# A clustered attention and two gated MLPs on one core: the first head pair's preparation laid out anew

## The chip, the cores and the metric

The kernel runs on one core of a Trainium2 chip. Its engines have a queue each: TensorE (PE, with its weight loads listed apart as PEld), VectorE (DVE), ScalarE (ACT), GpSimd (POOL), and SyncE (SP), which issues the DMAs here. An engine takes its own instructions in the order in which they were written, and waits for another by semaphores. The metric is the device time of one execution in microseconds (us).

## What is computed

Attention among tokens of one cluster, for 2 batches, 8 heads, 768 tokens and 64 columns per head, and behind it two MLPs on the 1536 x 512 result.

```python
q_assign = argmax(einsum('bhsd,hcd->bhsc', q_n, c_n))      # 16 centroids per head, all normalised
k_assign = argmax(einsum('bhsd,hcd->bhsc', k_n, c_n))
mask = q_assign[:, :, :, None] == k_assign[:, :, None, :]
scores = where(mask, scale * q @ k.T, -1e9)
attn = softmax(scores)
x = (attn @ v) as 1536 x 512
x = (sigmoid(x @ w_gate) * (x @ w_val)) @ w_out            # d_ff 1536
out = relu(x @ w_in2) ** 2 @ w_out2                        # d_ff 2048
```

## The kernel before

All operands of the matmuls are split into a high and a low part of a shorter float type (fp32r), so that two or three matmuls together keep nearly the accuracy of fp32. The engines' orders are written out by hand: the order of the calls in the program is the order on each queue.

**Attention** goes over 8 head pairs (2 batches x 4), a pair being two heads whose 64 columns together fill the 128 partitions. A pair has 12 units, `n` = 0 to 95 over all pairs; a unit is 128 query rows of one head against all 768 keys. Unit `n` takes: `scores` (four matmuls, two for each of two passes `a`, into a PSUM buffer `s`, of which there are two), the row maximum on DVE (`TENSOR_REDUCE`, L935, called the reduce below), the exponential with its row sum on ACT (L956), a 1e-9 added to the sum on POOL (L970), its reciprocal on DVE (L874), the normalisation on POOL (L875). Three units later (`LAG`) its six 128x128 blocks are transposed on PE (L821), copied to fp32r by ACT (`pt_hi`, L823), and DVE takes the rest (`pt_lo`, L829). The matmuls with `v` follow.

**The mask** is part of the score matmuls: the second pass has 16 more rows for each head, which hold a one-hot code of the token's cluster for `k` and minus a large number for `q`. So each pair needs a **preparation** before its units (`prep`): q and k are loaded with tokens on partitions and transposed (`tk0`, `tk1`, `tq0`, `tq1`: k or q, first or second half of the tokens); ACT writes the high part and DVE the low one (L568, L569); the similarities to the centroids are made (`sims`, L618: eight matmuls with the centroids as weights, then a copy by ACT, L624) and transposed back (`back`, L635; the tile `tot` sums their high and low part, L645); the best cluster is chosen by five DVE operations over `tot` (L656 to L679, the last writes the one-hot tile `oh`); `oh` is transposed and written as mask rows. `stack` issues DMAs that put parts of a head on the partitions where the score matmuls want them. The centroids are normalised once, at the start, and lie in `cen`.

The preparation of pair 0 stands before the loop, with some steps of pair 1's between (`STEPS` and `SECOND_STEPS` say at which unit a step of the next pair stands). `keep_warm` puts transposes of the identity on PE, whose result nobody reads. Head 0's mask rows of pair 0 are written straight to their place from PSUM by ACT and DVE (`first_mask`, L712 and L715); head 1's go to the tile `row` and from there by DMA, and are needed from unit 6 on.

What a step leaves to ACT and DVE (its `post`) is emitted later, when `drain` is called.

**The MLPs** are matmuls of 512 columns, with weights that are loaded as 64-bit floats and decoded on DVE and ACT.

## Time and profile before

| | |
|---|---|
| time, three runs | 820.73, 821.72, 821.74 us (median 821.72) |
| the profiled execution's own time | 821.03 us |
| its span, first to last instruction | 819.2 us |
| busy in the span | PE 803.1 us (98%), PEld 689.8, DVE 625.9 (76%), ACT 442.1 (54%), POOL 214.2 (26%) |
| chain that ended last | PE 80%, DVE 12%, POOL 3%, ACT 2%, DMA 1% |

The span and the profiled execution's time are of the same execution; 1.8 us lie outside the span. The busy time is an average over the opening, the attention (to about 275 us) and the MLPs. The chain is found by going back from the last instruction, at each step to what released it; where it names an engine, work on this engine, and nothing else, was what the end waited for.

### The profile page before, as it was taken

To read this page: it belongs to the slowest core of one execution; us is meant where nothing else is said; L and a number is where in the kernel's file an instruction comes from. 1 tells how busy PE (TensorE), PEld (TensorE's weight loads), DVE (VectorE), ACT (ScalarE), POOL (GpSimd) and SP (SyncE) were. 2 spreads that over 40 slices of the span, in tenths; PEclk is the share of its full clock that TensorE was granted. 3 is DMA by queue.
4 is the path that set the end of the run, shared out by engine and by line. 5 is a ranking of instruction groups with operands and counts; after the bars stand their busy time and mean duration, and the time that the engine had idled before them with its cause. 6 is when DMAs were issued, how large, how long until landed. Compare 5 with 4: busy or idle time off the path is not lost.

```text
span 819.2 us, 11691 instructions
## 1 busy us (share of the span) xinstructions
PE 803.1 (98%) x4097; PEld 689.8 (84%) x4097; DVE 625.9 (76%) x1144; ACT 442.1 (54%) x889; POOL 214.2 (26%) x349
## 2 busy tenths in 40 slices
PE   7899999999999999999999999999999999999998
PEld 6789989999998788888888888888888888888886
DVE  5899999999898378657878767769784787788233
ACT  5888889888896223532332223336745733642530
POOL 4668989988884200000000000000000000000000
PEclk9999999999999999999999999999999999999999
DMA  8465455364321122122221212202222212221012
GB/s 190 108 144 144 102 136 121 92 143 96 78 77 44 52 71 95 51 71 68 94 77 52 78 52 78 78 0 89 66 78 77 78 52 77 78 78 52 0 52 102
DMA packets 63274, 67.01 MB, mean 82 GB/s; under 512 B 28624, under 2 KB 54224, under 8 KB 63216
## 3 DMA queue, kind: packets, MB, share of 16 engines
q1 hardware_dynamic: 63216, 66.27, 29.3%
q8 instruction: 32, 0.52, 0.3%
q14 instruction: 26, 0.21, 0.1%
HBM read 45.12 MB, written 3.15 MB: 59 GB/s over the span
## 4 chain that ended last, share of the span: by engine, by line
PE 80%; DVE 12%; POOL 3%; ACT 2%; issue 1%; DMA 1%; SPq 0%; POOLq 0%; ACTq 0%; DVEq 0%
PE bank_b L427 18%; PE bank_a L350 13%; PE bank_a L351 13%; PE bank_a L349 13%; PE bank_a L427 9%; DVE pt_lo L829 4%; PE t L821 4%; DVE nm L935 3%; PE s L803 3%; PE o L839 2%; PE o L840 2%; POOL p L875 1%; PE t L618 1%; PE t L563 1%; PE o L888 1%
## 5 line engine op out<-in xcount | busy, mean ns | idle before, releaser
L350 PE MATMUL bank_a<-x_lo,w 128*128 128x512 f32 x480 | 187.0, 389 | 0.9 <-POOL x_lo L870 0.9
L349 PE MATMUL bank_a<-x_hi,w 128*128 128x512 f32 x480 | 186.9, 389 | 0.0
L351 PE MATMUL bank_a<-x_hi,w 128*128 128x512 f32 x480 | 186.9, 389 | 0.0
L393 DVE TENSOR_TENSOR slo<-act,shi 128x512 fp32r<-128x512 f32 x84 | 57.9, 689 | 66.8 <-ACT shi L392 60.3
L350 PEld LDWEIGHTS bank_a<-x_lo,w 128*128 128x128 f32 x480 | 90.1, 188 | 19.7 <-POOL x_lo L870 1.2
L349 PEld LDWEIGHTS bank_a<-x_hi,w 128*128 128x128 f32 x480 | 90.1, 188 | 18.8 <-POOL x_hi L868 0.2
L351 PEld LDWEIGHTS bank_a<-x_hi,w 128*128 128x128 f32 x480 | 90.1, 188 | 18.8
L829 DVE TENSOR_TENSOR pt_lo<-t,pt_hi 128x384 fp32r<-128x384 f32 x192 | 96.7, 546 | 5.4 <-ACT pt_hi L823 5.4
L875 POOL TENSOR_SCALAR p<-p,nm,ones 128x768 f32<-128x768 f32 x96 | 94.8, 988 | 15.7 <-DVE nm L874 15.3
L956 ACT ACTIVATE p<-s,nm 128x768 f32<-128x768 f32 x96 | 88.0, 917 | 15.9 <-DVE nm L874 10.8
L803 PE MATMUL s<-st_k,st_q 128*128 128x384 f32 (+1 forms) x384 | 91.0, 359 | 0.6 <-ACT p L956 0.5
L935 DVE TENSOR_REDUCE nm<-s 128x1 f32<-128x768 f32 x96 | 91.0, 948 | 0.0
L823 ACT CAST pt_hi<-t 128x384 fp32r<-128x384 f32 x192 | 83.2, 487 | 6.3 <-PE t L821 5.6
L821 PE MATMUL t<-ident,p 128*128 128x128 f32 x576 | 81.6, 275 | 4.3 <-DVE pt_lo L829 3.2
L392 ACT CAST shi<-act 128x512 fp32r<-128x512 f32 x84 | 51.7, 615 | 56.0 <-PE bank_b L427 32.9
L427 PE MATMUL bank_b<-wo,shi 128*128 128x512 f32 x256 | 78.8, 389 | 0.0
L231 ACT CAST w<-wtop 128x512 fp32r<-128x512 f32 x38 | 23.7, 623 | 101.8 <-DVE wtop L249 101.8
L821 PEld LDWEIGHTS t<-ident,p 128*128 128x128 f32 x576 | 66.2, 140 | 11.7 <-issue 4.2
L839 PE MATMUL o<-pt_hi,vt 128*128 128x384 f32 x192 | 65.1, 339 | 0.4 <-ACT oc L845 0.4
L375 DVE TENSOR_TENSOR act<-bank_a,sg 128x512 f32<-128x512 f32 x36 | 24.9, 691 | 53.1 <-PE bank_a L351 50.9
L803 PEld LDWEIGHTS s<-st_k,st_q 128*128 128x128 f32 (+1 forms) x384 | 62.5, 190 | 2.9 <-ACT p L956 2.2
L840 PE MATMUL o<-pt_lo,vt 128*128 128x384 f32 x192 | 64.7, 337 | 0.0
(137 smaller groups left out, 1386.2 us busy)
## 6 DMA issues: line engine op xcount, KB each, us to landing
wraw<-in_moe_w_out_dram SPq DMA_DIRECT2D x28, 512.0 KB, 3.2
wraw<-in_moe_w_in_dram SPq DMA_DIRECT2D x16, 512.0 KB, 3.7
wraw<-in_moe_w_gate_dram SPq DMA_DIRECT2D x11, 512.0 KB, 3.5
wraw<-in_moe_w_val_dram SPq DMA_DIRECT2D x11, 512.0 KB, 3.5
nat_v<-in_v_dram SPq DMA_DIRECT2D x8, 384.0 KB, 3.2
st_k<-st_k SPq DMA_DIRECT2D x16, 192.0 KB, 4.5
x<-oc SPq DMA_DIRECT2D x32, 96.0 KB, 2.1
out_dram<-part SPq DMA_DIRECT2D x12, 256.0 KB, 2.0
```

The costliest lines, as they stand in the source:

```text
L349: nc.tensor.matmul(bk, w[:, 0, ks], mov_hi[:, kk], start=(kk == 0), stop=False)
L350: nc.tensor.matmul(bk, w[:, 0, ks], mov_lo[:, kk], start=False, stop=False)
L351: nc.tensor.matmul(bk, w[:, 1, ks], mov_hi[:, kk], start=False, stop=(kk == KD - 1))
L427: nc.tensor.matmul(bk, st, mv, start=(first and n == 0), stop=(last and n == 2))
L803: nc.tensor.matmul(st[:, m, :NH], Q[i, e][: DEPTH[e][a], a, c * P : (c + 1) * P], K[i, e][: DEPTH[e][a], a, m * NH : (m + 1) * NH], start= ...
L821: nc.tensor.transpose(tp[:, m, :], Pt[u][:, c * P : (c + 1) * P], ident)
L823: nc.scalar.copy(hi, tp)
L829: nc.vector.tensor_tensor(out=lo, in0=tp, in1=f32(hi), op=ALU.subtract)
L839: nc.tensor.matmul(o, vt, hi[:, c, :], start=(c == 0), stop=False)
L875: nc.gpsimd.tensor_scalar(out=p, in0=p, scalar1=nm[:, 3:4], scalar2=ones, op0=ALU.mult, op1=ALU.mult)
L935: nc.vector.tensor_reduce(out=nms[n][:, 0:1], in_=st[n][:, :, :NH], axis=AX.XY, op=ALU.max, negate=True)
L956: nc.scalar.activation(out=e.rearrange("p (m n) -> p m n", m=2), in_=st.pop(n)[:, :, :NH], func=AF.Exp, bias=nms[n][:, 0:1], accum_out=nms ...
```

## The change

Everything that is changed stands before unit 4 of pair 0.

- Pair 0's q and k are loaded by one DMA each, in runs of 384 elements (1536 bytes) into the tile `spare`, instead of two DMAs each in runs of 64 elements (256 bytes) into `nat_k` and `nat_q`. Four copies (`by_token`) then put them by token: k's first half on DVE, q's first half on ACT, both second halves on POOL.
- The similarities of pair 0 are made by `compare`: 24 matmuls with the tokens as weights and 64 columns of `cen` as what moves, straight into the layout that `tot` needs. The eight matmuls of `sims`, the two copies by ACT and the six transposes back go.
- The choice and the masks are made by head (`of_head`). The five DVE operations run over head 0 alone (192 elements in a row of each partition in place of 384). Head 1's stand in the loop, at units 0 (`best1`), 1 (`same1`, one operation of which is on POOL) and 2 (`chosen1`); the transposes of its one-hot codes, one ACT operation and two DMAs stand at unit 3 (`mk`).
- The first score pass of units 0 and 1 (`score_pass` with `a` = 0, which needs no mask) stands ahead of the mask rows; the second halves of q's mask rows go from DVE to ACT, and the copies to `row` go from here.
- The centroids' squares are taken on DVE, not on ACT; `keep_warm` has 13, 6 and 2 transposes in place of 20, 8, 16 and 4; the zeros of pair 1's stack are written later; the table of Exp is loaded later.

```diff
-WARM = {-9: 8, -2: 16, -1: 4}
+BEGIN = [
+    "tk0", "tq0", "cen", "tk1", "tq1", "clear", "b0", "b1", "ka", "qa", "qb", "best", "exp", "same", "kb",
+    "-6", "early", "zeros", "-3", 6, "chosen", "-2", "first", "scores", "-1", 2,
+]
+FIRST_PAIR = {0: ["best1"], 1: ["same1"], 2: ["chosen1"], 3: ["mk"]}
...
+            def by_token(nm, n):
+                cs = slice(n * HB, (n + 1) * HB)
+                out, src = nat_t[0, nm][:, cs], whole[nm].rearrange("p h c d -> p c h d")[:, cs]
+                if n == 1:
+                    copy(out, src)
+                elif nm == "k":
+                    nc.vector.tensor_copy(out, src)
+                else:
+                    nc.scalar.copy(out, src)
...
+                    elif i == 0:
+                        raw = f32(spare[:, (2 + "kq".index(nm)) * S :][:, :S]).rearrange("p (h c d) -> p h c d", h=2, c=NB)
+                        nc.sync.dma_start(
+                            out=raw.rearrange("p h c d -> p h (c d)"), in_=src.rearrange("p h c d -> p h (c d)")
+                        )
...
+                def compare(bp, n):
+                    w = cen[:, 4 * hp + 2 : 4 * hp + 4].rearrange("p a c -> p (a c)")
+                    for x, nm in enumerate("kq"):
+                        for c in range(HB):
+                            at = slice((n * HB + c) * P, (n * HB + c + 1) * P)
+                            to = bp[:, c, x].rearrange("p b c -> p (b c)")
+                            nc.tensor.matmul(to, hi_t[nm][:, at], w, start=True, stop=False)
+                            nc.tensor.matmul(to, lo_t[nm][:, at], w, start=False, stop=True)
...
+                    def same():
+                        t = keep["tot"].rearrange("p b t c -> p (b t) c")[:, :, sl]
+                        eq = keep["eq", e] = keep["all"][:, e * NE : (e + 1) * NE]
+                        mx = keep["mx", e]
+                        nc.vector.tensor_tensor(out=eq, in0=t, in1=mx[:, :, None].to_broadcast([P, NE, NCL]), op=ALU.is_equal)
+                        (nc.gpsimd if e else nc.vector).tensor_tensor(
+                            out=eq, in0=eq, in1=first[:, None, :].to_broadcast([P, NE, NCL]), op=ALU.mult
+                        )
...
                         by_act(qt[:, :P], q, mts[0][:, :P])
                         by_dve(kt[:, NH:], k, mts[1])
                         by_act(kt[:, :NH], k, mts[0])
-                        by_dve(qt[:, NH:], q, mts[1])
                         by_act(qt[:, P:NH], q, mts[0][:, P:])
-                        by_dve(row[:, NH:], every, mts[1])
-                        by_act(row[:, :NH], every, mts[0])
-                        rows_out(row, slice(0, S))
+                        by_act(qt[:, NH:], q, mts[1])
...
-            keep_warm(20)
-            cd = centroid_prep()
...
+            keep_warm(13)
+            cd = centroid_prep()
+            for x in BEGIN:
+                if isinstance(x, int):
+                    keep_warm(x)
...
+                elif x == "scores":
+                    firsts = [ps_s.tile([P, 2, 512], F32, name="s") for _ in range(2)]
+                    for n in range(2):
+                        score_pass(units[n], firsts[n], 0)
+                elif x in prep0:
+                    do(prep0[x])
+                    drain()
+                else:
+                    for f in prep1.pop(int(x)):
+                        do(f)
+            drain()
+            score_pass(units[0], firsts[0], 1)
```

How the change moves instructions is seen at three places. The first is DVE, from the last of the five choosing operations (`oh`) to the third reduce. Before (names `st_k_143`, `x_lo_67` belong to pair 1's preparation, `st_k_136` and `st_q_138` to pair 0):

```order
L679 TENSOR_TENSOR oh<-eq,m_296 128x384
L569 SCALAR_TENSOR_TENSOR st_k_143<-t,st_k_143 128x384
L569 SCALAR_TENSOR_TENSOR x_lo_67<-t,st_q_145 128x384
L715 TENSOR_SCALAR st_k_136<-t,rscale,rbias 16x384
L715 TENSOR_SCALAR st_q_138<-t,rscale,rbias 16x384
L715 TENSOR_SCALAR row<-t,rscale,rbias 64x384
L935 TENSOR_REDUCE nm<-s 128x1
L569 SCALAR_TENSOR_TENSOR st_k_143<-t,st_k_143 128x384
L935 TENSOR_REDUCE nm<-s 128x1
L569 SCALAR_TENSOR_TENSOR x_lo_67<-t,st_q_145 128x384
L874 RECIPROCAL nm<-nm 128x1
L935 TENSOR_REDUCE nm<-s 128x1
```

And DVE with the change, from behind the mask rows on to the fourth reduce (L1037 is the reduce, L596 the low part, L954 the reciprocal; L756, L762, L769 and L770 are head 1's choice, L684 is the sum into `tot` of pair 1):

```order
L596 SCALAR_TENSOR_TENSOR st_k_143<-t,st_k_143 128x384
L1037 TENSOR_REDUCE nm<-s 128x1
L596 SCALAR_TENSOR_TENSOR x_lo_67<-t,st_q_145 128x384
L756 TENSOR_REDUCE mx<-tot 128x12
L1037 TENSOR_REDUCE nm<-s 128x1
L954 RECIPROCAL nm<-nm 128x1
L762 TENSOR_TENSOR eq<-tot,mx 128x192
L1037 TENSOR_REDUCE nm<-s 128x1
L954 RECIPROCAL nm<-nm 128x1
L684 TENSOR_TENSOR tot<-t,part 128x192
L769 TENSOR_REDUCE m_273<-eq 128x12
L770 TENSOR_TENSOR oh<-eq,m_273 128x12x16
```

The low part of pair 1's k (second half) went from behind the first reduce to ahead of it, that of its q from behind the second reduce to ahead of it, and four operations of head 1's choice stand between the reduces.

The second place is ACT, from the mask rows to the second exponential. Before:

```order
L712 ACTIVATE st_q_138<-t,rbias,rscale 16x128
L712 ACTIVATE st_k_136<-t,rbias,rscale 16x384
L712 ACTIVATE st_q_138<-t,rbias,rscale 16x256
L712 ACTIVATE row<-t,rbias,rscale 64x384
L568 ACTIVATE st_k_143<-t 128x384
L956 ACTIVATE p,nm<-s,nm 128x768
L624 COPY sim<-t 128x384
L568 ACTIVATE st_q_145<-t 128x384
L956 ACTIVATE p,nm<-s,nm 128x768
```

With the change:

```order
L790 ACTIVATE st_q_138<-t,rbias,rscale 16x128
L790 ACTIVATE st_k_136<-t,rbias,rscale 16x384
L790 ACTIVATE st_q_138<-t,rbias,rscale 16x256
L790 ACTIVATE st_q_138<-t,rbias,rscale 16x384
L595 ACTIVATE st_k_143<-t 128x384
L1061 ACTIVATE p,nm<-s,nm 128x768
L651 COPY sim<-t 128x384
L595 ACTIVATE st_q_145<-t 128x384
L1061 ACTIVATE p,nm<-s,nm 128x768
```

ACT's own order is as it was, with one piece of q's mask rows in the place of the copy to `row`.

The third place is PE at the comparison. Before:

```order
L618 MATMUL t<-x_hi_66,cen 128x384
L888 MATMUL o<-ident 128x128 x8
L635 MATMUL t<-ident,sim 128x128 x6
L563 MATMUL t<-ident,spare 128x128 x6
L888 MATMUL o<-ident 128x128 x16
```

With the change, its last six (L663 and L664 are the high and the low part of the tokens, x_hi_66 is q's low part of pair 0):

```order
L663 MATMUL t<-cen,st_q_138 128x64
L664 MATMUL t<-cen,x_hi_66 128x64
L663 MATMUL t<-cen,st_q_138 128x64
L664 MATMUL t<-cen,x_hi_66 128x64
L590 MATMUL t<-ident,spare 128x128 x3
L976 MATMUL o<-ident 128x128 x6
```

The transposes back of `sim` are gone, and so are the eight transposes of the identity that stood ahead of them.

## Rows read from the trace of the kernel before

**Rows 1.** Windows: busy us (instructions) by engine, granted clock, DMA share, GB/s
```profile
24.00:48.00 24.00, 21.60 (x140) 18.02 (x139) 22.41 (x49) 19.86 (x46) 17.30 (x26) 1.00 0.37 80
48.00:72.00 24.00, 23.04 (x159) 21.78 (x158) 23.02 (x48) 20.91 (x49) 17.95 (x26) 1.00 0.64 141
```

**Rows 2.** Chain that ended last, opening, in order of time: start, us, what
```profile
9.00 1.89 PE t L618 x8
...
13.67 0.56 DVE mx L656
...
16.30 0.56 DVE oh L679
...
59.60 0.92 PE t L821 x6
```

**Rows 3.** Timeline, all engines, opening: start, us, instruction [idle before <-releaser]
```profile
1.34 4.53 PE L888 MATMUL o<-ident 128*128 128x128 f32 x20 [1.34 <-POOL ident masks.py:199]
...
6.68 0.87 ACT L568 ACTIVATE st_k<-t 128x384 fp32r<-128x384 f32 x2 [0.87 <-PE t L563]
...
8.62 0.23 DVE L540 TENSOR_TENSOR cen<-t,cen 64x64 fp32r<-64x64 f32 x1 [0.27 <-ACT cen L539]
...
10.73 1.03 PE L888 MATMUL o<-ident 128*128 128x128 f32 x8
...
17.36 0.45 ACT L712 ACTIVATE st_q<-t,rbias,rscale 16x128 fp32r<-16x128 bf16 x1 [3.35 <-PE t L709]
...
19.68 0.47 ACT L568 ACTIVATE st_k<-t 128x384 fp32r<-128x384 f32 x1
19.80 0.94 DVE L935 TENSOR_REDUCE nm<-s 128x1 f32<-128x768 f32 x1
...
21.13 0.94 DVE L935 TENSOR_REDUCE nm<-s 128x1 f32<-128x768 f32 x1
...
22.03 0.50 ACT L568 ACTIVATE st_q<-t 128x384 fp32r<-128x384 f32 x1
...
22.56 0.56 DVE L569 SCALAR_TENSOR_TENSOR x_lo<-t,st_q 128x384 fp32r<-128x384 f32 x1 [0.49 <-ACT st_q L568]
```

**Rows 4.** Timeline of DVE, units 2 to 8
```profile
23.11 0.94 DVE L935 TENSOR_REDUCE nm<-s 128x1 f32<-128x768 f32 x1
25.05 0.94 DVE L935 TENSOR_REDUCE nm<-s 128x1 f32<-128x768 f32 x1
...
27.88 0.95 DVE L935 TENSOR_REDUCE nm<-s 128x1 f32<-128x768 f32 x1
...
32.91 0.95 DVE L935 TENSOR_REDUCE nm<-s 128x1 f32<-128x768 f32 x1
...
38.12 0.56 DVE L673 TENSOR_REDUCE m<-eq 128x24 f32<-128x384 f32 x1 [0.30 <-POOL eq L666]
```

**Rows 5.** DMA issues, first 30 us: tile, count, KB each, median us to landing
```profile
nat_q<-in_q_dram SPq DMA_DIRECT2D x4, 192.0 KB, 4.0
...
st_k<-row SPq DMA_DIRECT2D x1, 48.0 KB, 3.5
```

**Rows 6.** Tile nat_v: its DMAs' issue times, ns min/median/max, and landing
```profile
L492 SPq DMA_DIRECT2D nat_v<-in_v_dram x8: 377/377/802, 7.6 to 218.1; - x8
...
DMA to landing us min/median/max: 2.9/3.2/4.4
```

**Rows 7.** Groups by form, first 24 us: shapes, count | busy us, mean ns
```profile
L618 PEld LDWEIGHTS t<-st_k,cen 128*128 128x128 f32 x8 | 1.4, 189 | 0.4 <-PE t L563 0.4
...
L645 DVE TENSOR_TENSOR tot<-t,part 128x192 f32<-128x192 f32 x2 | 0.7, 358 | 2.8 <-ACT part L644 2.8
L635 PEld LDWEIGHTS t<-ident,sim 128*128 128x128 f32 x6 | 0.7, 141 | 0.0
...
L644 ACT COPY part<-t 128x192 f32<-128x192 f32 x2 | 0.6, 318 | 1.2 <-PE t L635 0.7 <-DVE tot L645 0.5
```

**Rows 8.** Costliest groups of the page: the exponential on ACT
```profile
L956 ACT ACTIVATE p<-s,nm 128x768 f32<-128x768 f32 x96 | 88.0, 917 | 15.9 <-DVE nm L874 10.8
```

More of the change, by code (lines that the diff above doesn't have):

```diff
@@ L725, in post @@
                         by_act(kt[:, :NH], k, mts[0])
[L726 removed]
                         by_act(qt[:, P:NH], q, mts[0][:, P:])
[L728 to L730 removed]
+                        by_act(qt[:, NH:], q, mts[1])
                     return post
                 if i == 0:
[L735 to L753 removed]
+                    h0, h1 = of_head(0), of_head(1)
+                    return {
+                        "tk0": transposes("k", 0),
+                        "tk1": transposes("k", 1),
+                        "tq0": transposes("q", 0),
+                        "tq1": transposes("q", 1),
+                        "b0": back(0),
+                        "b1": back(1),
+                        "ka": stack("k", 0),
+                        "qa": stack("q", 0),
+                        "kb": stack("k", 1),
+                        "qb": stack("q", 1),
+                        "clear": clear,
+                        "best": h0[0],
+                        "same": h0[1],
+                        "chosen": h0[2],
+                        "best1": h1[0],
+                        "same1": h1[1],
+                        "chosen1": h1[2],
+                        "first": first_mask,
+                        "mk": mask,
+                    }
                 acts = {
@@ L879, in cluster_attention_two_mlps, with zeros @@
             load(0, "v")
-            for nm in "kq":
-                for x in range(2):
+            nc.vector.memset(cen.rearrange("p a c -> p (a c)").bitcast(mybir.dt.int32), 0)
+            centroid_lengths()
+            for n in range(2):
+                for nm in "kq":
+                    by_token(nm, n)
+            def zeros(x):
+                for nm in "kq":
                     nc.gpsimd.memset(stacks[nm, 1, x][: D - NCL, 1].bitcast(I32), 0)
+            zeros(0)
             warm = ps_o.tile([P, NH], F32, name="o")
@@ L924, in cluster_attention_two_mlps @@
                     todo.setdefault(at, []).append(group)
-            st[0] = scores(units[0])
+            st[0] = firsts[0]
+            for m, x in FIRST_PAIR.items():
+                todo.setdefault(m, []).append([prep0[y] for y in x])
             for n in range(N + LAG + 4):
@@ L951, in cluster_attention_two_mlps @@
                     t1, h1 = evac(w, 1)
-                if n + 1 < N:
+                if n == 0:
+                    st[1] = firsts[1]
+                    score_pass(units[1], firsts[1], 1)
+                elif n + 1 < N:
                     st[n + 1] = scores(units[n + 1])
```

118 lines of the change are left out of this document (67 added, 51 removed).

## The prediction

> **What bounds the kernel now.** I read the windows first [rows 1]: behind the opening, from 24 to 72 us, DVE is busy 22.41 and 23.02 of 24 us and PE 21.60 and 23.04, so neither has much room. The chain in order of time says which one counts [rows 2]. Its opening runs through PE (the centroid matmuls from 9.00), through the five choosing operations on DVE from 13.67 to the end of `oh` at 16.86, and then, unit after unit, mostly through DVE, until it goes over to PE at 59.60 and stays there. DVE's timeline [rows 4] shows why: from about 27 us on it does one instruction after the other, and the longest stop that I find before 50 us is the 0.30 at 38.12. So a delay of DVE at unit 6 (its reduce starts at 32.91) arrives at 59.60, and from there at the end, nearly whole; so would a gain. What the change is worth is therefore read at one place, the start of unit 6's reduce, behind which DVE's order is the same in both kernels.
>
> The way from the opening to that place has two parts. Up to 16.86 each wait is a chain of small steps. From 16.86 the reduces start at 19.80, 21.13, 23.11, 25.05, 27.88 (units 0 to 4) and 32.91 (unit 6) [rows 3, 4]: that is 2.94 us behind `oh`, and then 1.33, 3.31, 5.25, 8.08 and 13.11 us behind the first reduce.
>
> **The change, step by step.**
>
> *Loading and transposes (9.00 before).* A load of 192 KB in short runs took 4.0 us to land [rows 5], and q is two such loads, issued behind k's two. One load of 384 KB in long runs takes 0.38 us to issue and at best 2.9 us to land [rows 6]. With k issued at 1.17 it lands at about 4.1; q, issued at 1.6 and behind k's bytes, I put at 4.9 (4.5 if k's bytes cost it nothing; 5.6 if the landings are like the median and q's bytes come wholly behind k's). Then q's first half waits for ACT's copy (0.48, like its other passes over 384 elements [rows 3]), for three transposes (0.9 at the slow rate at which k's began before: from 5.77 to ACT's start at 6.68 [rows 3]), ACT's high part (0.5), DVE's low part (0.55), and the back-and-forth of four small operations on `cen` (0.2 each, three of them behind the low part, with gaps 0.7 [rows 3]): 4.9 + 0.5 + 0.95 + 0.5 + 0.55 + 0.7 = 8.1, so that the comparison starts at 8.2. **-0.8** (-1.2 to -0.1).
>
> *The comparison.* Before: from 9.00 to the second `tot` at 13.64, 4.64 us, 1.03 of which PE spends on transposes that nobody reads [rows 3]. Now 24 matmuls, each with a weight load of its own. No matmul of such a narrow moving part stands in this trace. From below: eight transposes of 128 columns in 1.03 us, 0.11 apart once the last one's tail is taken off. From above: a load of fp32r weights is recorded with 189 ns, where that of a transpose has 141 [rows 7]; if nothing overlaps, 0.19. I take 0.12, near the transposes, since their loads too are hidden in that spacing: 24 x 0.12 + 0.25 for the tail, then ACT's copy 0.32, `tot` 0.36 [rows 7] and gaps of 0.1: 3.9. **-0.7** (-1.0 at 0.11, +0.9 at 0.19). The Trainium skill ("TensorE: Matmul & The Clock Gate", section "LDWEIGHTS (loading the stationary operand)") gives a load's time as its columns over 1.2 GHz, 107 ns for 128; by that the 24 would take 2.6 us, the step would be -1.0 and the sum 0.3 lower. The trace has no row that shows it alone.
>
> *The choice.* Five operations took 3.22 us from 13.64 to 16.86. An operation of 192 elements in a row takes 358 ns [rows 7] and one of 384 takes 560 [rows 2], a ratio of 0.64: 2.1 us now. **-1.1** (-1.4 to -0.9). So `oh` ends at 16.86 - 2.6 = 14.2. The loading of Exp's table stands on ACT under this stretch and costs nothing as long as ACT is done with pair 1's two high parts by then; I count 0.1 over, which DVE's first low part covers.
>
> *From `oh` to the first reduce.* Here the order turns against the change. ACT starts the mask rows 0.50 behind `oh` and does four pieces; in the place of the copy to `row` stands an equal piece of q's. Behind them is pair 1's high part of k: 19.68 before, 2.82 behind `oh`, 0.47 long [rows 3]. Before, the first reduce stood ahead of the low part that needs it; now it stands behind. So: 2.82 + 0.47, then 0.48 for the low part until the reduce can follow: 3.77 in place of 2.94, although DVE has lost two mask pieces. **+0.83** (+0.7 to +1.0). PE is not what is late: the second pass needs k's rows from ACT and DVE, there at 1.7 behind `oh`.
>
> *From the first reduce to unit 6's.* Times behind the first reduce. DVE's next instruction is now the low part of pair 1's q; it waits for ACT's high part, which stands behind the first exponential and a copy and started at 2.23 behind the reduce (22.03), ended at 2.73. Before, that wait stood behind the second reduce (22.56 [rows 3]). Now the low part ends at 3.3, `best1` takes 0.35 by the ratio above, and **the second reduce starts at 3.5, not 1.33**. Queued behind it are the reciprocal that releases the first normalisation on POOL, and the second exponential. The third starts after reciprocal and `same1`, at 4.8 (3.31). The fourth now stands behind pair 1's `tot`, whose copy on ACT stands behind the third exponential (0.92 [rows 8], its sum 0.2): 4.8 + 0.96 + 1.2 + 0.3 + 0.36, then two of `chosen1`, 0.7: 8.2 (5.25). The fifth stands behind two `pt_lo` and the second `tot`, which waits in the same way for the fourth exponential: 8.2 + 0.96 + 1.3 + 0.4 + 0.3 of decoding = 11.1 (8.08). From there to unit 6's reduce I take the 5.03 us of before: ACT has a new piece there, head 1's rows, and DVE has one `tot` less. Unit 6's reduce starts at 16.1, not 13.11. **+3.0** (+2.4 to +3.7). Of this only 1.4 us are the four operations that moved in; the rest is DVE waiting for ACT in places where it had a reduce to do.
>
> The other edits lie beside: the copies by token on POOL run while the first halves are handled; the zeros moved on POOL end long before the head-1 stack is read; squares on DVE come in a stretch where DVE has nothing else; the warming transposes are not on the path except as told below. On SP, the DMA that stacks k for head 1 goes ahead of pair 2's loads, and head 1's row DMAs behind pair 1's four stacking DMAs; those are out by 5 behind the first reduce, and the rows are written at 12, so SP keeps nobody waiting.
>
> **Sum.** -0.8 - 0.7 - 1.1 + 0.8 + 3.0 = **+1.2 us** at unit 6. DVE has at most the 0.30 to give back, and that stop is a wait for POOL that moves along. Against the profiled execution's own 821.03 us that is 822.2; the median of the three runs stands 0.7 above it, so on their scale 822.9. I predict 822.5, between the two.
>
> **The rivals.**
>
> *The comparison on a slow TensorE.* The windows print a granted clock of 1.00, but the first twenty transposes took 4.53 us, 0.227 each [rows 3], twice the 0.11 of those at 10.73: the levels of 1.2 and 2.4 GHz. It rose after PE had been at work without a break from 1.34 on, at about 6.4, among k's transposes. Now PE has 13 transposes, then gaps until k and q are there. If the clock stays low through the comparison, 24 x 0.1 us and 0.4 for the second halves come on top: +2.8, and 0.19 apart at full clock comes to +1.7; the sum is +2.9 to +4.0, 824 to 825.5. The Trainium skill says in "TensorE: Matmul & The Clock Gate", Part 1, that the clock is held low until the engine has been busy and falls again when it idles; by that rule the shortened warming works against the change, as this rival has it.
>
> *Faster: the delay is not carried.* If what the end waits for between 33 and 59.6 us is PE's amount of work and not DVE's, the late reduces are caught up, and the first unit's head start counts: -2.6 + 0.8 = -1.8, 819.3 to 820. PE had 2.4 us idle in the 24 us from 24 [rows 1], which is what could take it in. Against it: PE's idle time stands where it waits for DVE, and DVE has only 1.6 idle there, most of it ahead of unit 4's reduce. It decides if DVE's reduce of unit 6 starts later than 32.9 and the end is earlier all the same.
>
> *Head 1's mask rows come late.* They are written at about 12 behind the first reduce and go out in two DMAs, the second issued 0.65 later; at 3.5 to land [rows 5] they are there at 16.1, and the scores of unit 6 are wanted at 15.3. That adds up to 0.8: 823.3.
>
> *No change at all in the opening's length:* if q lands only at 5.6, -0.8 becomes -0.1: +1.9, 823.1.
>
> **How the numbers follow.** A measurement of this kernel tells about 0.2%, 1.6 us, from no change. My likeliest case, +1.2 with its own terms' errors, has 0.5 and lies mostly inside that bound, with a quarter of it above. The slow or unlapped comparison has 0.2 and is slower; late rows or late q 0.1, split; the faster rival 0.2, of which a part stays within the bound. Together: faster 0.17, same 0.45, slower 0.38. The range runs from the faster rival's 819.9 to 825.0, the middle of the slow comparison; the likeliest case's own range is 821.2 to 824.2.
>
> **What will show it.** Right: the comparison starts near 8.2, `oh` ends near 14.2, the reduces start at 18.0 and then 3.5, 4.8, 8.2 and 11.1 behind, unit 6's at 34.1, and DVE waits for ACT ahead of the second reduce for more than 1.5 us. Wrong: a second reduce less than 2 us behind the first, matmuls of the comparison more than 0.16 apart, a unit-6 reduce before 32, or a DVE that stands idle for more than 1 us between 34 and 60, through which a delay could be given back.

## The result, and the profile after

The changed kernel takes 826.81 us (median of four runs, 826.01 to 827.03) against 821.34 (820.73 to 821.74) of the kernel before, run beside it: a ratio of 1.0065 (95% interval 1.0048 to 1.0083). It is slower by 5.5 us, outside the range forecast. The profiled execution took 826.71 us with a span of 824.9, 5.7 more than before.

The windows that answer to [rows 1], and two more (busy us and instructions of each engine, granted clock, DMA share, GB/s):

```profile
9.00:18.00 9.00, 8.80 (x43) 8.23 (x42) 4.39 (x12) 4.14 (x9) 4.87 (x7) 1.00 0.35 89
...
24.00:48.00 24.00, 20.06 (x116) 17.10 (x115) 20.24 (x44) 17.29 (x40) 15.12 (x23) 0.86 0.37 85
48.00:72.00 24.00, 23.42 (x163) 21.88 (x163) 23.78 (x50) 21.05 (x50) 17.39 (x28) 1.00 0.62 133
...
26.00:32.00 6.00, 4.84 (x18) 4.64 (x19) 3.51 (x11) 3.72 (x9) 4.03 (x7) 0.50 0.51 116
```

From 24 to 48 us DVE does 44 instructions where it did 49, and TensorE's granted clock is 0.86, with a stretch at 0.50 inside; from 48 on both engines are as full as before. So what was lost was lost ahead of 48. Where exactly, the timeline shows (start, us, instruction, idle before); the rows answer to [rows 3, 4]:

```profile
1.34 3.03 PE L976 MATMUL o<-ident 128*128 128x128 f32 x13 [1.34 <-POOL ident masks.py:199]
...
4.60 0.55 DVE L493 COPY nat_k<-spare 128x384 f32<-128x384 f32 x1 [1.68 <-DMA spare<-in_k_dram]
...
5.89 2.08 DVE L551 TENSOR_SCALAR cd<-cn,css 128x64 f32<-128x64 f32 x2
6.00 0.51 ACT L495 COPY nat_q<-spare 128x384 f32<-128x384 f32 x1 [2.85 <-DMA spare<-in_q_dram]
...
6.05 0.51 POOL L565 TENSOR_SCALAR nat_q<-spare 128x384 f32<-128x384 f32 x1 [0.80 <-DMA spare<-in_q_dram]
...
6.50 0.74 POOL L968 MEMSET st_k<- 48x768 int32 x1
...
7.18 0.74 POOL L968 MEMSET st_q<- 48x768 int32 x1
...
9.55 0.42 PE L663 MATMUL t<-cen,st_k 128*128 128x64 f32 x1
...
9.78 0.40 PE L664 MATMUL t<-cen,st_k 128*128 128x64 f32 x1
...
14.48 0.40 PE L664 MATMUL t<-cen,x_hi 128*128 128x64 f32 x1
...
15.38 1.49 PE L976 MATMUL o<-ident 128*128 128x128 f32 x6
...
17.30 0.36 DVE L770 TENSOR_TENSOR oh<-eq,m 128x192 bf16<-128x192 f32 x1
...
19.51 0.49 PE L590 MATMUL t<-ident,spare 128*128 128x128 f32 x3
...
21.64 0.95 DVE L1037 TENSOR_REDUCE nm<-s 128x1 f32<-128x768 f32 x1
...
24.41 0.56 DVE L596 SCALAR_TENSOR_TENSOR x_lo<-t,st_q 128x384 fp32r<-128x384 f32 x1 [1.82 <-ACT st_q L595]
...
25.14 0.95 DVE L1037 TENSOR_REDUCE nm<-s 128x1 f32<-128x768 f32 x1
...
29.89 0.36 DVE L684 TENSOR_TENSOR tot<-t,part 128x192 f32<-128x192 f32 x1 [2.15 <-ACT part L683]
...
30.82 0.95 DVE L1037 TENSOR_REDUCE nm<-s 128x1 f32<-128x768 f32 x1
...
38.64 0.95 DVE L1037 TENSOR_REDUCE nm<-s 128x1 f32<-128x768 f32 x1
```

The 24 small matmuls start 4.93 us apart from first to last, 0.214 each. The transposes around them took 0.23 each (13 in 3.03) and 0.25 (6 in 1.49); those at 19.51 took 0.16 (3 in 0.49, tail included). TensorE was on its lower level from the start through the whole comparison. The profile prints 1.00 there: ahead of the first change that it records, the column tells nothing.

By the prediction's steps, from the start of the span to unit 6's reduce (38.64; before 32.91):

| step | forecast | measured | where read |
|---|---|---|---|
| comparison starts | -0.8 | +0.55 | 9.55, before 9.00 |
| comparison | -0.7 | +1.44 | to the end of `tot` at 15.63: 6.08, before 4.64 |
| choice | -1.1 | -1.19 | `oh` ends at 17.66: 2.03, before 3.22 |
| `oh` to first reduce | +0.83 | +1.04 | 3.98, before 2.94 |
| first reduce to unit 6's | +3.0 | +3.89 | 17.00, before 13.11 |
| sum | +1.2 | +5.73 | |

The span grew by 5.7, so the delay at unit 6 was carried whole, as forecast. Of the chain (start, us, what), which answers to [rows 2], it is enough to see that it goes over to PE for good 6.06 us later than before, and that head 1's mask rows stand on it:

```profile
35.17 2.22 DMA st_q<-row
...
43.16 1.01 POOL eq L705
...
65.66 0.92 PE t L901 x6
```

In the kernel before, the chain at the place of the second of these rows was this, also on POOL:

```profile
34.57 0.99 POOL p L875
...
37.08 1.02 POOL eq L666
```

### The profile page after: what moved, and what is told of

The parts are those of the page before. It is cut to its first block, busy times and chain, and to the rows that moved or that the text cites. A ratio compares the mean times of both kernels' runs of the same rounds, so it can differ in the third digit from the quotient of the medians.

```text
span 824.9 us, 11669 instructions
## 1 busy us (share of the span) xinstructions
PE 807.2 (98%) x4086; PEld 694.3 (84%) x4086; DVE 626.7 (76%) x1150; ACT 441.1 (53%) x886; POOL 215.7 (26%) x352
## 4 chain that ended last, share of the span: by engine, by line
PE 78%; DVE 12%; ACT 4%; POOL 3%; DMA 1%; issue 1%; SPq 0%; ACTq 0%; POOLq 0%; DVEq 0%
PE bank_b L431 18%; PE bank_a L354 13%; PE bank_a L355 13%; PE bank_a L353 13%; PE bank_a L431 9%; DVE pt_lo L909 4%; DVE nm L1037 4%; PE s L878 3%; PE t L901 3%; PE o L919 2%; PE o L920 2%; POOL p L955 1%; ACT p L1061 1%; ACT pt_hi L903 1%; PE t L645 1%
## 5 line engine op out<-in xcount | busy, mean ns | idle before, releaser
L1061 ACT ACTIVATE p<-s,nm 128x768 f32<-128x768 f32 x96 | 88.1, 918 | 18.3 <-DVE nm L954 10.6
L878 PE MATMUL s<-st_k,st_q 128*128 128x384 f32 (+1 forms) x384 | 93.0, 364 | 4.1 <-ACT p L1061 3.4
L1037 DVE TENSOR_REDUCE nm<-s 128x1 f32<-128x768 f32 x96 | 91.1, 949 | 0.0
```

The source lines that it names most:

```text
L878: nc.tensor.matmul(st[:, m, :NH], Q[i, e][: DEPTH[e][a], a, c * P : (c + 1) * P], K[i, e][: DEPTH[e][a], a, m * NH : (m + 1) * NH], start= ...
L1037: nc.vector.tensor_reduce(out=nms[n][:, 0:1], in_=st[n][:, :, :NH], axis=AX.XY, op=ALU.max, negate=True)
L1061: nc.scalar.activation(out=e.rearrange("p (m n) -> p m n", m=2), in_=st.pop(n)[:, :, :NH], func=AF.Exp, bias=nms[n][:, 0:1], accum_out=nms ...
```

## The experiments

Three causes could explain the 4.5 us that were not forecast and the 3.8 that were forecast behind `oh`: TensorE's clock; POOL holding DVE; the order on DVE. No run changes the loads of k and q, so what their landing costs is read from the profiles alone. Kernels whose names begin with b_ are edits of the kernel before, the others of the changed one. All times are medians (of a_reduces_first2 there is one run), and the difference is to the kernel before, run beside each.

| kernel | us | to before | `oh` ends | first reduce behind it | 2nd, 4th, unit 6's behind the first |
|---|---|---|---|---|---|
| before | | | 16.86 | 2.94 | 1.33, 5.25, 13.11 |
| after | 826.81 | +5.5 | 17.66 | 3.98 | 3.50, 9.18, 17.00 |
| a_warm20 | 823.69 | +2.8 | 17.21 | 3.98 | 3.49, 9.18, 16.92 |
| a_zeros_first | 825.58 | +4.7 | 17.03 | 3.97 | 3.50, 9.19, 16.92 |
| a_reduces_first | 823.87 | +3.0 | | | |
| a_reduces_first2 | 826.03 | +4.9 | 17.50 | 3.36 | 1.60, 7.08, 16.34 |
| a_all_three | 822.11 | +1.3 | 14.34 | 4.33 | 1.60, 7.05, 16.10 |
| a_more_warm | 826.37 | +5.5 | 14.02 | 3.81 | 3.49, 9.06, 16.79 |
| a_all_warm | 823.15 | +2.3 | 15.72 | 4.11 | 1.60, 7.06, 16.23 |
| b_warm21 | 820.86 | 0.0 | 16.29 | 3.63 | 1.33, 5.26, 13.13 |
| b_low_first | 822.89 | +2.1 | 16.20 | 3.80 | 3.24, 6.95, 15.07 |
| b_small2 | 821.16 | 0.0 | 17.07 | 4.19 | 1.33, 5.27, 13.14 |
| a_old_compare | 823.34 | +2.4 | 15.12 | 2.69 | 1.59, 7.06, 16.37 |
| a_early1 | 820.06 | -0.9 | 14.22 | 3.84 | 1.33, 5.23, 13.07 |
| a_early1_old | 821.28 | +0.3 | 15.11 | 4.16 | 1.34, 5.24, 13.07 |
| a_early1_w13 | 824.63 | +3.5 | 17.10 | 3.89 | 1.33, 6.37, 14.11 |
| a_early1_warm | 822.21 | +1.0 | 16.32 | 5.86 | 1.33, 6.58, 14.75 |
| a_best | 819.88 | -1.0 | 15.23 | 3.50 | 1.33, 5.26, 13.12 |

The places are those of one profiled execution each, and where the clock falls at another moment from one execution to the next, that one is not the median.

**One cause at a time in the changed kernel.**

```
-            keep_warm(13)
+            keep_warm(20)                                # a_warm20

+            zeros(0)                                     # a_zeros_first: ahead of by_token
...
-            zeros(0)

-            drain()                                      # a_reduces_first, a_reduces_first2
             score_pass(units[0], firsts[0], 1)
...
-                todo.setdefault(m, []).append([prep0[y] for y in x])
+                todo.setdefault(m, [[]])[0].extend(prep0[y] for y in x)
```

*a_warm20.* 

> The changed kernel with 20 warm-up matmuls, as before, in place of 13. Theory (TensorE's clock): the shorter warm-up leaves TensorE at its lower level through the comparison, which costs about 2.5 us there; with 20 the comparison's matmuls stand 0.13 us or less apart (0.21 now), its work ends 2 to 2.5 us earlier, and the total is 823.3 to 825.0. Rival (the spacing belongs to such small matmuls): they stay 0.21 apart at either level, and the total stays within 0.4 us of 826.8, or rises where the longer warm-up delays the first transposes.

The median of 823.69 lies in the clock theory's span, and four of the five runs took 822.66 to 824.48; the profiled one took 826.40, and its work of the comparison ended only 0.45 us earlier. Its rows on PE show one reason:

```profile
9.27 0.30 PE L663 MATMUL t<-cen,st_k 128*128 128x64 f32 x1
9.40 0.34 PE L664 MATMUL t<-cen,st_k 128*128 128x64 f32 x1
9.55 0.40 PE L663 MATMUL t<-cen,st_k 128*128 128x64 f32 x1
9.76 0.40 PE L664 MATMUL t<-cen,st_k 128*128 128x64 f32 x1
```

The clock had risen, and fell while the first matmuls ran: 0.13 apart, then 0.21. The spacing is thus a matter of the level, not of the matmul, and the rival falls. But a longer warm-up alone does not hold the level; it fell a second time in this execution, from 26.5 to 30.0.

*a_zeros_first.* 

> The changed kernel with POOL's memsets of zeros moved ahead of its copy of q, so that POOL has less left to do while VectorE prepares the centroids. Theory (VectorE is held while POOL works): the two small subtractions end near 6.7 to 7.2 us in place of 7.97, the comparison starts at 8.6 to 8.9 in place of 9.55, and the total falls by 0.6 to 0.9. Rival (they are slow by themselves or wait for a transfer): they still end at about 7.9, and the total stays within 0.3 us.

The two subtractions for `cd` take 0.42 us here in place of 2.08,

```profile
5.49 0.42 DVE L551 TENSOR_SCALAR cd<-cn,css 128x64 f32<-128x64 f32 x2
```

the comparison starts at 8.92 (9.55), and `oh` ends 0.64 earlier. So they are not slow by themselves, and the rival falls. That moving the memsets is what freed them is not shown: in a_warm20 and a_reduces_first2, where the memsets stand as in the changed kernel, they took 0.42 as well. What differs is when q lands. In the changed kernel POOL's copy of q started at 6.05 and the second subtraction at 6.06, and this one took 1.91; in the three profiles with 0.42 it was under way before the copy started, or done. In a_more_warm, with the memsets in their old place, the two took 0.67 and ended with POOL's copy alone. What the long hold costs, the path from ACT's copy of q to the comparison tells: 3.55 in the changed kernel, 3.26 in three others that were at the lower level and without the long hold (a_zeros_first, a_reduces_first2, a_early1_w13), so 0.29. The rest of the 0.64 is q, which had landed 0.34 earlier. Against the kernel before, run beside each, the total falls by 0.75, which the intervals don't tell from nothing (1.0042 to 1.0075 here). The Trainium skill ("SBUF — State Buffer", section "SBUF: two separate sides") says of a pair of ports that POOL shares with DVE instructions of certain modes, or with two inputs in SBUF (these only against a POOL instruction that reads SBUF): the instruction that starts first has the pair for its whole length, and the other is blocked. The trace agrees as to the keeping out; but the second subtraction ended at 7.97, 0.05 behind the last of three POOL instructions in a row, so it was held for longer than one.

*a_reduces_first and a_reduces_first2.* 

> The changed kernel with pair 1's low parts and head 1's work put behind the first reduces on VectorE, where the kernel before has them: k's low part behind the first reduce, q's behind the second. Theory (the order on VectorE costs the time behind the one-hot): first reduce 2.9 to 3.1 us behind the one-hot's end (3.97 now), the second 1.3 to 1.7 behind it (3.50 now), unit 6's reduce 14 to 15 behind the first (17.0 now), total 823.3 to 824.3. Rival (only the work added counts, wherever it stands): unit 6's reduce stays 16 to 17 behind the first, and the total falls by 0.5 us at most.

> The same kernel as a_reduces_first, for a profile: the changed kernel with only pair 1's low parts and head 1's steps put behind the first reduces. First reduce 2.9 to 3.3 us behind the one-hot where the clock is up there, else about 4; second 1.3 to 1.7 behind the first, fourth 7.0, unit 6's 15.5 to 16.2 as with the three edits together; total 822.3 to 825.

The total fell by 2.5, to 823.87, inside the span of the theory of the order. The places are those of a_reduces_first2, one execution of the same kernel, which took 826.03: more than was expected of it, and more than the six others that took 822.31 to 825.16. In it the second reduce stands 1.60 behind the first, as the theory had it; but unit 6's stands 16.34 behind, the rival's 16 to 17, and not 14 to 15. This execution had its comparison at the lower level, and a second stretch there from 29.9 to 36.7. So the gain in total is shown, and that the second reduce comes back; what keeps unit 6 back even with the reduces first was open here.

*a_all_three.* 

> The three edits together: 20 warm-up matmuls, zeros ahead of the copy of q on POOL, the low parts behind the first reduces. If the three causes are separate and add up (2 to 2.5, 0.7 and 2.5 to 3.5 us), the total is 819.8 to 821.5, level with the kernel before or up to 1.5 us under it. If two of them are one cause, or another wait takes their place (the mask rows of head 1 for unit 6, or a later fall of the clock), 822 to 824.

Against the kernel before, run beside each, the three edits gain 2.6, 0.75 and 2.5 singly, and 4.2 together: not additive, the second outcome. The comparison now ran at the upper level, 24 matmuls in 2.59 us from 8.70, 0.113 apart, and `oh` ended at 14.34 (forecast in the prediction: 14.2). Then the clock was down from 12.2 to 19.0 and from 29.2 to 32.6.

**Order on DVE, in the kernel before.**

```
+            drain()
             st[0] = scores(units[0])
...
+                if n == 0:
+                    drain()
                 for part in decoding.pop(n, []):
```

*b_low_first.* 

> The kernel before with one thing of the change: pair 1's low parts stand ahead of the first reduces on VectorE, k's ahead of the first and q's ahead of the second. Theory (the order on VectorE costs the time behind the one-hot): first reduce 3.6 to 3.9 us behind the one-hot's end (2.94 now), second 3.0 to 3.6 behind the first (1.33 now), unit 6's reduce 14.5 to 16.5 behind the first (13.11 now), total 822.3 to 824.5. Rival (the slack of those units takes it up, and the time is lost by head 1's work alone): first reduce later by 0.8 at most, unit 6's reduce as before, total within 0.5 us of the kernel before.

The theory held: a ratio of 1.0022 (1.0013 to 1.0031) from the place of two operations that exist in both kernels.

```profile
19.52 0.56 DVE L569 SCALAR_TENSOR_TENSOR st_k<-t,st_k 128x384 fp32r<-128x384 f32 x1 [0.30 <-ACT st_k L568]
20.00 0.95 DVE L936 TENSOR_REDUCE nm<-s 128x1 f32<-128x768 f32 x1
22.76 0.56 DVE L569 SCALAR_TENSOR_TENSOR x_lo<-t,st_q 128x384 fp32r<-128x384 f32 x1 [1.82 <-ACT st_q L568]
23.24 0.95 DVE L936 TENSOR_REDUCE nm<-s 128x1 f32<-128x768 f32 x1
...
26.95 0.96 DVE L936 TENSOR_REDUCE nm<-s 128x1 f32<-128x768 f32 x1 [1.13 <-PE s L803]
```

The wait of 1.82 for ACT is to the digit that of the changed kernel at 24.41. ACT's high part stands behind the first exponential, and DVE now stops for it with a reduce at hand. This profile, too, has a stretch at the lower level, from 25.2 to 28.5: the fourth reduce, the last line, waited 1.13 for scores that took PE 1.65 there and 0.97 at 22.02, at the upper level. So up to 0.7 of the 1.96 by which unit 6's reduce is late may be the clock's. The second reduce is late by 1.91 ahead of that stretch, and the two of the ten executions with a mean clock of 1.00 took 822.15 and 823.46, both above every one of the 29 of the kernel before (820.0 to 821.89): the order costs time without the clock.

**What lets the clock fall.**

```
-            keep_warm(13)                                # a_more_warm
+            keep_warm(20)
-    "-6", "early", "zeros", "-3", 6, ... "-1", 2,
+    "-6", "early", "zeros", "-3", 14, ... "-1", 4,
+                keep_warm({1: 2, 3: 12}.get(n, 0))

-WARM = {-9: 8, -2: 16, -1: 4}                            # b_warm21 (and 13 for 20 at the start)
+WARM = {-9: 0, -2: 6, -1: 2}
```

*a_more_warm.* 

> The changed kernel with 52 warm-up matmuls in place of 21: 20 at the start (13 before this edit), 14 in place of 6 during the choice, 4 in place of 2 ahead of head 1's scores, 2 and 12 where TensorE stood idle while head 1's mask rows were made; nothing else is changed. Theory (TensorE's clock): at the full level the comparison's matmuls stand 0.11 apart, the comparison takes 2.4 us less, the scores behind the one-hot take 0.95 us a unit in place of 1.65, and there is no second fall; total 822.5 to 824.0. If the idle stretches while the centroids are prepared still let the clock fall, as with 20 alone: 823.5 to 825.5. Rival (the clock is of no account, the order on VectorE is all): within 0.5 us of 826.8, or above it by what the warm-up work delays.

The theory missed: the median is 826.37, within the rival's 0.5 of 826.8. But the rival's reason is wrong. Three runs at a mean granted clock of 0.990 to 0.993 took 825.4 to 828.3; the profiled one, at 1.00 throughout, took 822.68, so the clock is of great account, and the added matmuls did not hold it. That one execution is, but for the 31 matmuls more, the changed kernel without its clock trouble, and it comes out as the prediction's kernel: `oh` at 14.02, first reduce at 17.83, unit 6's at 34.62 (forecast 14.2, 18.0, 34.1), total 822.68 (822.5).

*b_warm21.* 

> The kernel before with the changed kernel's 21 warm-up matmuls: 13, 6 and 2 in place of 20, 8, 16 and 4; nothing else is changed. Theory (the change lost time by cutting the warm-up): the clock rises late or falls within the first 35 us, the comparison's eight matmuls of 384 columns take longer, and the total rises by 1.0 to 4.0 us. Rival (it is the change's small matmuls and its new order that let the clock fall): the clock stays up, total within 0.4 us of the kernel before.

The rival's total won: with the 21 warm-up matmuls of the changed kernel the old order loses nothing (0.9999, 0.9991 to 1.0008). But the clock did not stay up. The first two matmuls of the comparison took 0.80 (0.59 before), so 13 left the level low up to there, and in the profile it was down again from 16.5 to 19.9, where the first reduce came 3.63 behind `oh` and not 2.94. Against that, without the eight transposes that nobody reads it is 3.87 from the start of the comparison to `tot`, not 4.64. The two nearly cancel: the first reduce starts at 19.92, before at 19.80.

*b_small2* (the comparison by 64 columns in the kernel before, both halves ahead of the stacking transfers):

```
+                        if i == 0:
+                            compare(bp, n)
...
-                        sims(0),
-                        sims(1),
+                        back(0),
+                        back(1),
                         stack("k", 0),
```

> The kernel before with only the comparison of the first pair done as in the changed kernel, ahead of the transfers that stack its rows: 24 matmuls of 64 columns in place of eight of 384, a copy and six transposes. All 48 warm-up matmuls stay, 8 of them behind the comparison. Theory (the small matmuls let the clock fall): they run 0.11 apart, the one-hot ends 1.0 to 2.0 us earlier, the clock falls within 5 us of the comparison, and at most 0.8 us of the gain is left at unit 6's reduce: total 820.2 to 821.8. Rival (idle stretches do it): the clock stays up, the gain is kept whole: total 818.9 to 819.9.

The theory of the small matmuls held in half of the executions. Three of the ten at a mean clock of 1.00 took 819.3 to 819.8, the gain that the rival promised; five at 0.995 took 821.8 to 822.4. The profile is one of the latter (822.24):

```profile
10.37 0.28 PE L636 MATMUL t<-cen,st_q 128*128 128x64 f32 x1
10.48 0.28 PE L637 MATMUL t<-cen,x_hi 128*128 128x64 f32 x1
10.59 0.36 PE L636 MATMUL t<-cen,st_k 128*128 128x64 f32 x1
10.76 0.40 PE L637 MATMUL t<-cen,st_k 128*128 128x64 f32 x1
10.97 0.40 PE L636 MATMUL t<-cen,st_k 128*128 128x64 f32 x1
...
13.11 1.97 PE L898 MATMUL o<-ident 128*128 128x128 f32 x8
```

The level falls at 10.6 in the middle of a row without a gap, and stays down through 12 small matmuls, 8 warm-up ones and six transposes, until 17.5. A first form of this kernel (b_small, 828.46) had the comparison behind the stacking transfers, so that it waited for them and read rows already stacked; it answers nothing. The Trainium skill ("TensorE: Matmul & The Clock Gate", Part 1) has the clock fall after idling. Here PE's row shows no idle time from 9.26 on, and the measurement decides: small matmuls back to back did not keep it up. PE had stood idle ahead of them, 0.43 us before 7.91 and 0.17 before 9.26; but so it had in the kernel before (0.69 before 7.82 and 0.17 before 9.00), whose comparison in 384 columns kept the level. What in the small matmuls does it, their columns or their weight loads, no run tells.

*a_old_compare* (a_all_three with `"s0", "s1", 8, "b0", "b1"` in place of `"b0", "b1"`, that is with matmuls of 384 columns). 

> The changed kernel with the three edits of the fourth run (20 warm-up matmuls, zeros first, reduces first) and the comparison of the kernel before: eight matmuls of 384 columns, a copy and six transposes, with 8 warm-up matmuls between. Theory (the small matmuls let the clock fall): the clock stays up to the first reduce; the one-hot ends at 15.3 to 16.2 (14.34 with the small matmuls), the first reduce comes 2.9 to 3.3 behind it (4.33), total 820.8 to 822.3 against 822.1. Rival (the idle stretches do it): the clock falls here too before 20 us, and the total is 823 or more.

Half right. In the profile the clock stayed up past the first reduce, which came 2.69 behind `oh`; then it was down from 28.1 to 34.9, where head 1's rows are made. The median of 823.34 lies above the theory's 820.8 to 822.3, and the runs (821.6 to 825.8) are no better than those of a_all_three.

*a_all_warm* (a_all_three with the warm-up matmuls of a_more_warm). 

> The three edits of the run before it (20 warm-up matmuls, zeros first, reduces first) with the further warm-up matmuls of the first kernel of this call. There the clock fell at 12.2 to 18.6 us and at 29.1 to 32.6, the first reduce came 4.33 us behind the one-hot, and unit 6's reduce 16.1 behind the first. Theory: with the clock up the first reduce comes 2.9 to 3.2 behind the one-hot and unit 6's reduce 14.5 to 15.5 behind the first, 32.0 to 33.2 in the span; total 820.0 to 821.3, level with the kernel before. If the clock falls all the same or the added matmuls delay the first scores: 821.5 to 823. Rival (head 1's separate choice and its late mask rows cost what is left): total 822 or more with the clock at its upper level throughout.

Two kinds of execution again: four of twelve at a clock of 0.999 or 1.00 took 820.5 to 821.1, as the theory had it, the rest 823.0 to 824.3; in the profile the clock fell at 10.4, inside the comparison.

**What was left behind the first reduce.** In every kernel so far with the reduces first, the fourth reduce came 7.05 to 7.08 behind the first, not 5.25, and in all four profiles (a_reduces_first2, a_all_three, a_all_warm, a_old_compare) the clock was up between the two, in a_all_three from 0.3 us behind the first. So it was not the clock.

```
-    ... "first", "scores", "-1", 2,
+    ... "first", "scores", "best1", "same1", "chosen1", "-1", 2,
-FIRST_PAIR = {0: ["best1"], 1: ["same1"], 2: ["chosen1"], 3: ["mk"]}
+FIRST_PAIR = {1: ["mk"]}
```

*a_early1* (a_all_three with this). 

> The fourth run's kernel (20 warm-up matmuls, zeros first, reduces first) with head 1's choice ahead of the first reduce, in the 2.55 us that VectorE waits there, and head 1's mask rows made at step 1 in place of 3. Theory (what is left of the loss behind the first reduce is head 1's work between the reduces): the fourth reduce comes 5.2 to 5.7 behind the first (7.05 now), unit 6's 13.1 to 14.3 (16.1 now), total 819.0 to 821.0. Rival (the clock's second fall or the pressure on TensorE is what costs there): unit 6's reduce stays 15.5 or more behind the first, total 821.7 to 823.

```profile
15.88 0.35 DVE L756 TENSOR_REDUCE mx<-tot 128x12 f32<-128x192 f32 x1
...
17.79 0.36 DVE L770 TENSOR_TENSOR oh<-eq,m 128x192 bf16<-128x192 f32 x1
18.06 0.95 DVE L1036 TENSOR_REDUCE nm<-s 128x1 f32<-128x768 f32 x1
...
31.13 0.94 DVE L1036 TENSOR_REDUCE nm<-s 128x1 f32<-128x768 f32 x1
```

All its numbers were met. Head 1's choice fills the wait of DVE ahead of the first reduce, and behind it every reduce stands where it did before, to 0.05 us. 820.06 is 0.9 under the kernel before (0.9993, 0.9983 to 1.0003), which the interval doesn't tell from nothing; against a_all_three the gain is 2.1.

*a_early1_w13* (13 warm-up matmuls in it). 

> The kernel with head 1's choice ahead of the first reduce, with 13 warm-up matmuls at the start in place of 20; nothing else is changed. Theory (the 13 do not raise the clock): the comparison's matmuls stand 0.21 apart, the one-hot ends 2.3 to 3.2 us later than with 20 (14.22), the total is 2 to 3.2 us higher: 822.0 to 823.3. Rival (the warm-up's length is of no account once the rest is mended): within 0.6 us of it, 819.5 to 820.7.

4.6 us, more than expected: `oh` 2.88 later, unit 6's reduce 1.04 more behind the first (a second stretch at the lower level, 24.5 to 27.9), and in this execution a third at about 277 to 281 us.

*a_early1_old* (384 columns in it) and *a_early1_warm* (16 and 4 warm-up matmuls for 6 and 2). 

> The run before it with the comparison of the kernel before (eight matmuls of 384 columns). If the small matmuls cost more by the clock than they save: total 818.8 to 820.5, under the run before it and under the kernel before. If they save what they promise (1.4 us at the upper level): total 0.5 to 1.5 above the run before it.

> The kernel with head 1's choice ahead of the first reduce (20 warm-up matmuls, zeros first, reduces first) with 16 warm-up matmuls during the choice in place of 6, and 4 in place of 2 ahead of the first scores. There the clock fell at 15.7 and rose at 19, and the first reduce came 3.84 us behind the one-hot. Theory: with the clock up it comes 3.0 to 3.3 behind it, and the total is 818.7 to 819.8, 0.1 to 0.25 per cent under the kernel before. If the clock falls earlier for another reason, or the matmuls added delay the one-hot's transposes: 820 to 822.

With 384 columns the total is 1.2 higher, the second outcome; the clock still fell, at 15.9, 0.7 us behind the end of 2.00 us in which PE stood idle ahead of the mask rows. In a_old_compare the same idle time, to 15.17, was not followed by a fall until 28.1, so it is not enough to explain one. With 64 columns and more warm-up six of twelve runs took 819.4 to 820.6 at a clock of 0.999 or 1.00, near the theory's span, and six 823.9 to 826.7, above all that was expected. Neither alone holds the clock.

*a_best* (both, and head 1's product with `first` on DVE). 

> The kernel of a_early1_old (20 warm-up matmuls, zeros first, reduces first, head 1's choice ahead of the first reduce, comparison by matmuls of 384 columns) with 16 warm-up matmuls during the choice and 4 ahead of the first scores as in the kernel before, and head 1's comparison with the mask of firsts on VectorE in place of POOL, whose 0.78 us of waiting stood in the choice. Theory: the clock stays up, the first reduce comes 2.9 to 3.2 us behind the one-hot (15.1), at 18.0 to 18.4, unit 6's 13.1 behind it, and the total is 819.0 to 820.0, 0.1 to 0.3 per cent under the kernel before, with little spread. If the clock falls all the same: 821 or more in some of the runs.

```profile
8.00:18.00 10.00, 8.81 (x67) 7.95 (x68) 6.73 (x19) 7.14 (x15) 5.66 (x9) 1.00 0.67 163
18.00:24.00 6.00, 4.73 (x31) 3.96 (x30) 4.51 (x11) 4.54 (x11) 2.85 (x6) 1.00 0.60 147
24.00:48.00 24.00, 21.96 (x145) 18.65 (x144) 23.21 (x50) 20.24 (x49) 16.60 (x25) 1.00 0.47 100
```

These windows have a clock of 1.00 throughout, and all eleven runs lie between 819.49 and 820.85: 0.9986 of the kernel before (0.9977 to 0.9995), and under both kernels. The first reduce came later than expected (3.50 behind `oh`), since DVE does head 1's choice until 18.8; unit 6's stands at 31.85, 1.06 ahead of before. With the comparison and the warm-up matmuls (20, 8, 16 and 4) of the kernel before, what is left of the change here is its loads, its choice by head and its early score passes; how the 1.0 us divides among them is not shown.

## Why the prediction was wrong

Two steps failed: the landing of q, and TensorE's level in the comparison, which decided.

*Loading (-0.8; came out +0.55).* The term that failed is the landing of q: "4.9 (4.5 if k's bytes cost it nothing; 5.6 if ...)". ACT's copy of it started at 6.00, and in the other profiles of changed kernels at 5.34 to 6.62; so the bound of 5.6 was too low as well. Why it lands then is open. Behind that the path was 3.55 for 3.3 reckoned, and 0.29 of it is POOL holding DVE, whose moved work the step had priced at nothing. At the upper level that path took 2.91 (a_all_three) and 2.92 (a_more_warm).

*The comparison (-0.7; came out +1.44).* This is the step that decided, with 2.1 of the 4.5 us. The spacing of 0.12 was right for the upper level (0.113 in a_all_three); the error was to price the step at that level and to give the slow clock, the rival that came true, a chance of 0.2. The matmuls came 0.214 apart, at the lower level from the first to the last. The profile had the sign: thirteen transposes instead of twenty, and a rise before only at about 6.4. The rival's size, +2.8, was about right: between a_early1_w13 and a_early1 the comparison up to `tot` differs by 2.46 (6.08 and 3.62), and `oh` by 2.88. The range ended at 825.0, inside this rival's own 824 to 825.5; 826.81 is above both, since q's landing came on top. What the prediction did not see is that the small matmuls let the clock fall even after a full warm-up, shown by b_small2.

*The choice (-1.1; -1.19)* and *`oh` to the first reduce (+0.83; +1.04)* were right. b_low_first shows the second alone (+0.86), and at the upper level it came to 3.81 for 3.77 (a_more_warm).

*First reduce to unit 6's (+3.0; +3.89).* The mechanism was right: second reduce at 3.50 as forecast, +1.96 at unit 6 in the kernel before with the low parts alone (up to 0.7 of it the clock's), all of it gone in a_early1. The size was off at the fourth reduce, 9.18 for 8.2. With the lower level, `tot` came 1.0 late. At the upper level, in a_more_warm, `tot` came when forecast (7.27 behind the first), but `oh` took 1.21 for 0.36 while POOL made `vt`, and the fourth reduce came at 9.06 all the same: unit 6's stands 16.79 behind the first there, 17.00 in the changed kernel. What the second stretch at the lower level costs by itself these two don't tell, since POOL's hold took its place in one of them.

*The rivals.* The delay was carried whole, so the faster rival fell. The reading by which it was to be carried was too simple, though: the chain does not run "mostly through DVE". In the kernel before it is mainly on POOL from 21.93 to 28.89 and from 34.57 to 38.10, and on PE and ACT from 40.85 to 48.9. Late mask rows did occur: they landed at 37.39, and unit 6's scores waited 0.63 for them. DVE had other work up to unit 6's reduce, so the 5.73 do not show this wait; but the chain comes through it, over PE and ACT to POOL's `eq`, and there the delay is 6.08 (43.16 for 37.08), some 0.3 more.

Open: why the executions of one kernel fall on one side or the other. The clock fell at 9.5, 10.4, 10.6, 11.0, 12.2 and 15.7, or not at all, in kernels with the same comparison; the kernel before shows something of it too (4 of 15 of its executions beside a_best took 822.0 to 822.7, the rest 819.8 to 821.6).

## What to carry to other kernels

Where TensorE is on the path of an opening, small matmuls and fewer warm-up ones can be paid for with the clock: price a stage at both levels, and look at the spacing of known instructions, not at the mean of the clock column. An instruction put ahead of a ready one on a full engine delays it by its wait as well as its length (a wait of 1.82 us ahead of 0.56 here). Work split off from a choice belongs into a wait that the engine already has (2.55 us ahead of the first reduce in a_all_three), not between the instructions that it has ready.

## What was not expected of the hardware

- The granted clock fell from 1.0 to 0.5 in the middle of matmuls of 64 columns 0.113 apart, with no gap on PE's row (b_small2, 10.6 us).
- DVE's short operations on SBUF at times end only with POOL's: 2.08 us for 0.42 beside a copy and two memsets (the changed kernel), 0.67 ended with the same copy (a_more_warm, a_all_three), 1.21 for 0.36 beside an operation on 128x384 (a_more_warm, 25.75 to 26.75).
- One execution of a_reduces_first took 1627.02 us: the page shows TensorE 99% busy, and its groups of 512 columns at 674 ns, where in the kernel before they take 389. The row of the first of these groups (line, operation, count, busy us, mean ns):

```profile
L354 PE MATMUL bank_a<-x_lo,w 128*128 128x512 f32 x480 | 323.8, 674 | 0.0
```

By these times the clock was at the lower level for the whole program, and yet the mean granted clock printed 1.00. Why is open. The six other runs of this kernel took 822.31 to 825.16.
